# Loads of v in 20 and 10 columns, stores in pairs of pieces, and a new order for both

## The chip, the cores and the metric

The kernel runs on one core of a Trainium2 chip. The metric is the device time of one execution in microseconds; the median of several runs is given, and one further execution was profiled. TensorE is called PE here, VectorE DVE, ScalarE ACT, GpSimd POOL and SyncE SP.

## The reference

Four batches of channel attention (the attention matrix is 256 x 256, over channels), followed by a mixture of eight low-rank adapters of which each token uses two. The tokens are N = 6,400 per batch, C = 256 channels, r = 16.

```python
qn = q / (norm(q, axis=1) + 1e-06)            # q, k, v: (4, 6400, 256) f32, norms over tokens
kn = k / (norm(k, axis=1) + 1e-06)
s  = kn.transpose(0, 2, 1) @ qn / tau         # (4, 256, 256)
a  = softmax(s, axis=-1)
x  = (v @ a).reshape(25600, 256)
logits = x @ w_gate                           # (25600, 8); the two largest per token
w = softmax(of the two)
out = x + sum over the two of w * ((x @ A[e]) @ B[e])
```

The output is 25,600 x 256 in f32.

## The kernel before

**Tiling.** The tokens of a batch are laid out as 128 partitions x 50 columns; a column is 128 tokens x 256 channels. q and k of a batch come in three loads each, of 17, 17 and 16 columns (`QK`); some are cut finer (`PARTS`). v of a batch is worked on in five pieces of ten columns (`PC`, `NP`), each with its own load. All these loads turn f32 into bf16 on the way and are issued by POOL (`do_load`, L627). The first four columns of q and k of batch 0 come as f32 from SP and ACT.

**Stages.** For each batch, PE accumulates over the 50 columns the Gram matrix of k and q and, beside it, the squares that the norms need (`G`, L642, L646, L651). Groups of columns named in `OFF` have their squares made on ACT and added on DVE instead (`sq`, `add`, `red`, L664 to L679). Then come the norms, the softmax and the product of its matrix with gate and adapter weights (`rsqrt` to `a`). Only then can a piece of v be finished: PE transposes it (`T`, L828), makes the gate logits (`log`, L866) and, behind the gate chain on DVE, the adapter product (`Z`, L919), or both at once where the piece is in `MERGED` (`ZL`, L852). The gated product is transposed (`gzT`, L942), and the output `Y` is made two columns at a time (L955, L960), copied to SBUF by ACT or DVE (`Ye`) and stored by SP (`do_store`, L971).

**Buffers.** `STORE` lists them: six buffers for q and k loads, three pieces of v side by side in one tile `VS`, four transposed pieces (`vT`), seven pieces of output in one tile `Y`, six PSUM banks for the stages, three sets of gate tiles. A load waits until every user of its buffer has finished, and the loads on POOL go out in the order written in `WORDS` (a word is q and k, or v, then the batch, then the part). A store may also be made to wait until a certain load has landed: `HOLD` names, for a piece, that load (batch, part; for v the piece). SP's queue is in order.

**Order.** The order on each engine is made when the kernel is built: `make_plan` writes down all steps with their dependences, their costs and a rank (the place of their load in `WORDS`; `AHEAD` and `SQ` shift ranks), and `Plan.run` plays them through with those costs and takes on each engine the best-ranked step that is ready. `Clock` is its notion of PE's clock; where PE would be idle, it puts `warm` matmuls (L818). The result is a fixed sequence for each engine. `V`, `PAIRS` and `SPLIT` are already in the code, but neutral: `V` has five loads of one piece for each batch, and the two others are empty.

Of the kernel before, what the change touches and what calls it, by code (L numbers as in the profile page):

```python
# [10 lines left out]
FP32 = mybir.dt.float32  # L11
I32 = mybir.dt.int32
BF16 = mybir.dt.bfloat16
# [19 lines left out]
class Clock:  # L33


    WINDOW, FIRST, LOW, HIGH = 3.413, 0.31, 0.55, 0.8

    def __init__(self):
        self.busy, self.cold = [0.0], [True]
# [23 lines left out]
        w = self.at(t)  # L63
        return t - self.FIRST - (w - 1) * self.WINDOW - self.busy[w] > self.SPARE

    SPARE = 0.8


class Plan:
# [171 lines left out]
PC = 10  # L241
NP = 5
UNITS = ((0, 4), (4, 4), (8, 2))
QK = ((0, 17), (17, 17), (34, 16))
V = (((0, 1), (1, 1), (2, 1), (3, 1), (4, 1)),) * 4
PAIRS = set()

GROUPS = ((0, 6), (6, 6), (12, 5), (17, 6), (23, 6), (29, 5), (34, 6), (40, 5), (45, 5))
ZUNITS = ((0, 3), (3, 3), (6, 2), (8, 2))
STORE = {"zl": 1, "bank": 6, "qk": 6, "v": 3, "vT": 4, "y": 7, "gate": 3, "gz": 4, "gzT": 4, "sq": 1, "ssq": 2, "port": 1}  # L250


def group_of(c):
# [187 lines left out]
def make_order(words):  # L441

    order = [("qk", 0, i) for i in range(len(QK))]
    for w in words.split():
# [1 line left out]
    return order  # L446


WORDS = ('q10 v00 v01 v02 q11 q12 v03 v04 v10 q20 v11 v12 q21 v13 q22 v14 q30 q31 v20 v21 v22 q32 v23 v24 v30 '
         'v31 v32 v33 v34')  # L450
HEAD = 5.05
COL = 1.024 * 1.17647 / 32
WARM = 150
AHEAD = 2.8

HOLD = {(0, 0): ('k', 2, 0), (0, 1): ('v', 3, 4), (0, 3): ('v', 2, 3), (1, 0): ('v', 3, 1), (1, 1): ('v', 3,
        1), (1, 3): ('v', 2, 3), (1, 4): ('v', 3, 0), (2, 2): ('v', 3, 2), (2, 3): ('v', 0, 4), (3, 0):
        ('k', 3, 2), (3, 1): ('k', 1, 1), (3, 2): ('v', 0, 1), (3, 4): ('k', 2, 1)}

PARTS = {(0, 0): ((0, 4), (4, 13)), (0, 2): ((34, 8), (42, 8)), (3, 2): ((34, 8), (42, 8))}  # L460
FINE = 2
SPLIT, SHARES = set(), ()
OFF = {(0, 0, 'k'), (0, 1, 'q'), (0, 2, 'q'), (0, 3, 'q'), (0, 5, 'q'), (0, 6, 'k'), (0, 8, 'k'), (1, 0,
        'k'), (1, 1, 'k'), (1, 2, 'k'), (1, 2, 'q'), (1, 3, 'q'), (1, 4, 'k'), (1, 5, 'q'), (1, 6, 'k'), (1,
        6, 'q'), (2, 0, 'k'), (2, 0, 'q'), (2, 3, 'q'), (2, 5, 'k'), (2, 5, 'q'), (2, 6, 'k'), (2, 7, 'q'),
        (2, 8, 'q'), (3, 0, 'k'), (3, 0, 'q'), (3, 1, 'q'), (3, 2, 'k'), (3, 2, 'q'), (3, 4, 'q'), (3, 5,
        'k'), (3, 6, 'k'), (3, 6, 'q'), (3, 7, 'k'), (3, 8, 'k')}
SQ = 0
SAFE = 0
MERGED = {(0, 1), (0, 4), (1, 0), (2, 1), (2, 2), (3, 0), (3, 2), (3, 3)}  # L470


def first_ahead(nc, names):
# [31 lines left out]
def kernel(  # L505
# [58 lines left out]
    def make_consts():  # L564
        ident = const.tile([P, P], BF16, name="ident")
        make_identity(nc, ident)
        W["ident"] = ident
        W["ident32"] = const.tile([P, P], FP32, name="ident32")
        nc.vector.tensor_copy(W["ident32"], ident)
        ones = const.tile([P, P], FP32, name="ones")  # L570
        nc.vector.memset(ones, 1.0)
        W["ones"] = ones
        neg = const.tile([P, 1], FP32, name="neg_inv_tau")
        nc.vector.memset(neg, -inv_tau)
        W["neg"] = neg
        W["zeros"] = const.tile([P, 256], BF16, name="zeros")
        nc.vector.memset(W["zeros"], 0.0)
        nc.scalar.activation(scrap[:, 0:1], neg[0:1, :], ACT.Exp)

    scrap = const.tile([1, 16], BF16, name="scrap")  # L580
# [128 lines left out]
    def do_rsqrt(s, b):  # L709
        n2 = st[b]["n2"]  # L710
        for x, w in enumerate("kq"):
            part = held.get(("bank", ("n2p", w, b)))
            if part is None:
                continue
            if all((b, g, w) in OFF for g in range(len(GROUPS))):
                nc.vector.tensor_copy(n2[:, x, :], part)
            else:
                nc.vector.tensor_tensor(out=n2[:, x, :], in0=part, in1=n2[:, x, :], op=OP.add)

        r = bat.tile([P, 2, CC], FP32, name="r0")  # L720
        nc.vector.tensor_scalar(out=r.bitcast(I32), in0=n2.bitcast(I32), scalar1=-0.5,
                                scalar2=float(0x5F1FFFF9), op0=OP.mult, op1=OP.add)
        for it, (c1, c0) in enumerate(((-0.703952253, 1.681914351), (-0.5, 1.5))):
            sq = bat.tile([P, 2, CC], FP32, name=f"sq{it}")
            nc.vector.tensor_tensor(out=sq, in0=r, in1=r, op=OP.mult)
            nc.vector.scalar_tensor_tensor(out=sq, in0=sq, scalar=c1, in1=n2,
                                           op0=OP.mult, op1=OP.mult)
            nxt = bat.tile([P, 2, CC], FP32, name=f"r{it + 1}")
            nc.vector.scalar_tensor_tensor(out=nxt, in0=sq, scalar=c0, in1=r,
                                           op0=OP.add, op1=OP.mult)  # L730
            r = nxt
        rqI = one.tile([P, CC, P], FP32, name="rqI")
        for ic in range(CC):
            nc.vector.tensor_scalar(out=rqI[:, ic, :], in0=W["ident"],
                                    scalar1=r[:, 1, ic:ic + 1], scalar2=None, op0=OP.mult)
        if inv_tau != 1.0:
            rt = bat.tile([P, CC], FP32, name="rt")
            nc.vector.tensor_scalar(out=rt, in0=r[:, 0, :], scalar1=inv_tau, scalar2=None, op0=OP.mult)
            st[b]["rk"] = rt
        else:  # L740
            st[b]["rk"] = r[:, 0, :]
        st[b]["rqI"] = rqI
# [72 lines left out]
        nc.scalar.copy(held["qk", (what, 0, 0), ""][:, 0:PARTS[0, 0][0][1], :], W[what])  # L815

    def do_warm(s, n):
        nc.tensor.matmul(bank(s, ("warm", n), [P, 512], FP32), W["ident"], W["zeros"][:, None, :].to_broadcast([P, 2, 256]),  # L818
                         start=True, stop=True)


# [16 lines left out]


    def gate_tiles(s, b, i):  # L840
        for part in ("log", "eq1", "lm", "t", "th", "mask", "g2"):
            sb(s, "gate", (b, i), [P, PC, E], FP32, part)
        for part in ("m1", "m2", "msum"):
            sb(s, "gate", (b, i), [P, PC], FP32, part)
# [30 lines left out]
    def gate_step(name):  # L875
        def f(s, b, i):
            if (b, i) in MERGED and name == "m1":
                gate_tiles(s, b, i)
            g = {part: held["gate", (b, i), part]
                 for part in ("log", "m1", "eq1", "lm", "m2", "msum", "t", "th", "mask", "g2")}  # L880
            if (b, i) in MERGED:
                g["log"] = held["zl", (b, i), ""][:, :, 0:E]
            wide = [P, PC, E]
            if name == "m1":
                nc.vector.tensor_reduce(out=g["m1"], in_=g["log"], axis=AX.X, op=OP.max)
            elif name == "eq1":
                nc.vector.tensor_tensor(out=g["eq1"], in0=g["log"], in1=g["m1"].to_broadcast(wide),
                                        op=OP.is_equal)
            elif name == "lm":
                nc.vector.scalar_tensor_tensor(out=g["lm"], in0=g["eq1"], scalar=-1e30, in1=g["log"],  # L890
                                               op0=OP.mult, op1=OP.add)
            elif name == "m2":
                nc.vector.tensor_reduce(out=g["m2"], in_=g["lm"], axis=AX.X, op=OP.max)
            elif name == "mask":
                nc.vector.tensor_tensor(out=g["mask"], in0=g["log"], in1=g["m2"].to_broadcast(wide),
                                        op=OP.is_ge)
            elif name == "msum":
                nc.vector.tensor_tensor(out=g["msum"], in0=g["m1"], in1=g["m2"], op=OP.add)
            elif name == "t":

                nc.vector.scalar_tensor_tensor(out=g["t"], in0=g["log"], scalar=2.0,
                                               in1=g["msum"].to_broadcast(wide),
                                               op0=OP.mult, op1=OP.subtract)
            elif name == "th":
                nc.scalar.activation(g["th"], g["t"], ACT.Tanh, scale=0.5)
            else:

                nc.vector.scalar_tensor_tensor(out=g["g2"], in0=g["th"], scalar=1.0, in1=g["mask"],
                                               op0=OP.add, op1=OP.mult)
        return f  # L910
# [13 lines left out]
    def do_Ze(s, b, i, u):  # L924
        c, n = UNITS[u]
        gz = sb(s, "gz", (b, i, u), [P, n, ER], BF16)
        z = held["zl", (b, i), ""][:, c:c + n, E:] if (b, i) in MERGED else held["bank", ("Z", b, i, u)]
        pairs = gz.rearrange("p c d -> p (c d)").rearrange("p (h x two) -> p h two x", two=2, x=ER)
        for h in range(n // 2):
            nc.vector.tensor_tensor(  # L930
                out=pairs[:, h].rearrange("p c (e r) -> p c e r", e=E),
                in0=z[:, 2 * h:2 * h + 2, :].rearrange("p c (e r) -> p c e r", e=E),
                in1=held["gate", (b, i), "g2"][:, c + 2 * h:c + 2 * h + 2, :].to_broadcast([P, 2, E, R]), op=OP.mult)

    def do_gzT(s, b, i, u):
        c, n = UNITS[u]
# [98 lines left out]
```

## Time and profile before

| | |
|---|---|
| median of 4 runs | 254.55 us (254.31 to 254.83) |
| profiled execution | 254.28 us, its span 252.5 us |
| granted PE clock, mean | 0.966 |
| PE busy | 221.2 us (88%) |
| DVE busy | 170.8 us (68%) |
| ACT busy | 158.4 us (63%) |
| loads by POOL (q0) | 38.80 MB written, 74.6% of 16 engines |
| stores by SP (q1) | 26.87 MB with the first pieces, 26.0% |
| HBM | 78.91 MB read, 26.21 MB written |

The time of an execution is a little more than its span, which runs from the first to the last instruction. A DMA share is the busy time of the 16 DMA engines; a load counts the bytes that it writes (bf16), so loads alone show about 215 GB/s and stores alone about 425.

### The profile page before, as it was taken

Reading aid. Unit: us, or ns where it says so; the run is one execution under the profiler, and the core shown is the slowest. Engines: PE = TensorE matmul, PEld = TensorE weight load, DVE = VectorE, ACT = ScalarE, POOL = GpSimd, SP = SyncE. Lnnn points to the kernel's source line nnn. Section 1 sums busy time; section 2 is a strip of 40 time slices with the busy share of each in tenths; the row PEclk is TensorE's granted clock in tenths of the full one; section 3 lists DMA queues with packets and bytes.
Section 4 is the critical chain, followed back from the end, with each engine's and each line's share of the span. In section 5 each row is a group of like instructions: output and inputs, shape, how many; then the busy total and the mean of one; then the engine's idle time right before and its main releaser. Section 6 shows DMA issues by size and latency. Waiting matters only on the chain.

```text
span 252.5 us, 6005 instructions
## 1 busy us (share of the span) xinstructions
PE 221.2 (88%) x2467; PEld 196.9 (78%) x2467; DVE 170.8 (68%) x485; ACT 158.4 (63%) x294; POOL 26.7 (11%) x54
## 2 busy tenths in 40 slices
PE   0775995899999899999998998899998889999970
PEld 0463883699899898889997997699978879999960
DVE  0024386169996988786749679879996797598430
ACT  5324123366877758767774778756953958877760
POOL 7003011011000201000101203010000110000000
PEclk9978899599999999999999999999999999999997
DMA  8999999999999999999999999999999999999995
GB/s 251 214 216 212 212 222 210 215 219 216 215 211 219 306 222 210 316 292 243 220 212 301 234 219 216 207 213 215 214 302 405 423 244 303 346 378 425 426 413 235
DMA packets 11147, 66.71 MB, mean 264 GB/s; under 512 B 1264, under 2 KB 1648, under 8 KB 6512
## 3 DMA queue, kind: packets, MB, share of 16 engines
q0 software_dynamic: 6912, 38.80, 74.6%
q1 hardware_dynamic: 3872, 26.87, 26.0%
q10 hardware_dynamic: 336, 0.66, 0.8%
q8 instruction: 19, 0.31, 0.4%
q14 instruction: 8, 0.07, 0.1%
HBM read 78.91 MB, written 26.21 MB: 416 GB/s over the span
## 4 chain that ended last, share of the span: by engine, by line
PE 56%; DMA 26%; DVE 9%; ACT 4%; issue 1%; POOL 0%; POOLq 0%; DVEq 0%
DMA qk<-in_k_dram 14%; PE Y_ps L955 14%; PE acc L642 8%; PE Y_ps L960 7%; DMA v<-in_v_dram 7%; PE T_ps L828 6%; DMA out_dram<-y 5%; PE gzT_ps L942 4%; PE Z_ps L919 4%; DVE ssq L670 4%; PE ZL_ps L852 3%; PE acc L646 2%; ACT sq L664 2%; PE acc L651 2%; PE log_ps L866 2%
## 5 line engine op out<-in xcount | busy, mean ns | idle before, releaser
L642 PE MATMUL acc<-qk 128*128 128x256 bf16 x400 | 74.8, 285 | 15.7 <-DMA qk<-in_k_dram 9.5
L955 PE MATMUL Y_ps<-a_bf,vT 128*128 128x256 bf16 x400 | 60.0, 272 | 0.9 <-ACT y L810 0.9
L670 DVE TENSOR_TENSOR ssq<-ssq,sq 128x1280 f32<-128x1280 f32 (+1 forms) x27 | 43.3, 1604 | 25.4 <-ACT sq L664 25.1
L810 ACT COPY y<-Y_ps 128x512 f32<-128x512 f32 x83 | 48.0, 588 | 18.8 <-PE Y_ps L960 12.0
L664 ACT ACTIVATE sq<-qk 128x1280 f32<-128x1280 bf16 (+1 forms) x27 | 36.9, 1368 | 28.1 <-DVE ssq L670 9.9
L642 PEld LDWEIGHTS <-qk 128*128 128x128 bf16 x400 | 35.8, 103 | 20.3 <-DMA qk<-in_k_dram 11.0
L955 PEld LDWEIGHTS <-vT 128*128 128x128 bf16 x400 | 38.7, 99 | 5.3 <-issue 1.0
L960 PE MATMUL Y_ps<-ball,gzT 128*128 128x256 bf16 x200 | 38.2, 273 | 0.0
L646 PE MATMUL acc<-qk 128*128 128x128 bf16 x210 | 30.0, 225 | 0.0
L651 PE MATMUL acc<-qk 128*128 128x128 bf16 x200 | 29.0, 229 | 0.0
L828 PE MATMUL T_ps<-ident,v 128*128 128x128 f32 x200 | 28.4, 277 | 0.0
L930 DVE TENSOR_TENSOR gz<-Z_ps,gateg 128x256 bf16<-128x256 f32 x60 | 22.4, 440 | 4.3 <-PE Z_ps L919 4.1
L810 ACT COPY vT<-T_ps 128x512 f32<-128x512 f32 (+1 forms) x43 | 21.7, 540 | 5.2 <-PE T_ps L828 4.9
L646 PEld LDWEIGHTS <-qk 128*128 128x128 bf16 x210 | 21.2, 101 | 3.0
L828 PEld LDWEIGHTS T_ps<-ident,v 128*128 128x128 f32 x200 | 22.5, 143 | 0.4 <-issue 0.2
L810 ACT COPY gzT<-gzT_ps 128x256 f32<-128x256 f32 (+1 forms) x45 | 14.7, 347 | 11.7 <-PE gzT_ps L942 11.6
L627 POOL DMA_DIRECT2D v<-in_v_dram x20 | 11.1, 553 | 102.4 <-PE T_ps L828 88.5
L960 PEld LDWEIGHTS <-gzT 128*128 128x128 bf16 x200 | 19.5, 98 | 2.5 <-DVE gzT L812 0.3
L942 PE MATMUL gzT_ps<-ident,gz 128*128 128x128 f32 x100 | 19.7, 281 | 1.4 <-DVE gz L930 1.0
L651 PEld LDWEIGHTS <-qk 128*128 128x128 bf16 x200 | 18.9, 103 | 2.4
L919 PE MATMUL Z_ps<-waA_sb,vT 128*128 128x128 bf16 x240 | 17.7, 219 | 0.0
L664 ACT ACTIVATE ssq<-qk 128x1536 f32<-128x1536 bf16 x8 | 11.9, 1486 | 8.4 <-DMA qk<-in_k_dram 4.3
(80 smaller groups left out, 274.0 us busy)
## 6 DMA issues: line engine op xcount, KB each, us to landing
out_dram<-y SPq DMA_DIRECT2D x18, 1280.0 KB, 12.6
v<-in_v_dram POOLq DMA_DIRECT2D x20, 640.0 KB, 25.1
qk<-in_q_dram POOLq DMA_DIRECT2D x7, 1088.0 KB, 22.2
qk<-in_k_dram POOLq DMA_DIRECT2D x7, 1088.0 KB, 26.8
qk<-in_q_dram POOLq DMA_DIRECT2D x4, 512.0 KB, 23.0
qk<-in_k_dram POOLq DMA_DIRECT2D x4, 512.0 KB, 24.7
qk<-in_q_dram POOLq DMA_DIRECT2D x2, 1024.0 KB, 30.9
qk<-in_k_dram POOLq DMA_DIRECT2D x2, 1024.0 KB, 35.2
```

What stands on the lines that cost most here:

```text
L642: nc.tensor.matmul(acc[ic][:, 0:256], kt[:, j, ic::CC], qt[:, j, :], start=c == 0, stop=False, skip_group_check=True)
L646: nc.tensor.matmul(acc[ic][:, 256:384], kt[:, j, ic::CC], kt[:, j, ic::CC], start=False, stop=False, skip_group_check=True)
L651: nc.tensor.matmul(acc[ic][:, 384:512], qt[:, j, ic * P:(ic + 1) * P], qt[:, j, ic * P:(ic + 1) * P], start=False, stop=c == NC - 1, skip_ ...
L664: nc.scalar.activation(out[:, 0:n, :], t[:, j:j + n, :], ACT.Square)
L670: nc.vector.tensor_tensor(out=t, in0=t, in1=held["sq", (w, b, g), ""][:, 0:n, :], op=OP.add)
L810: nc.scalar.copy(out, in_)
L828: nc.tensor.matmul(ps[:, j, :], vt[:, c + j, :].bitcast(FP32), W["ident32"], is_transpose=True, start=(j == 0), stop=(j == n - 1))
L919: nc.tensor.matmul(ps[:, j, :], vT_of(b, i, c + j)[:, :, ic], st[b]["aA"][:, ic, :], start=(j == 0 and ic == 0), stop=(j == n - 1 and ic = ...
L930: nc.vector.tensor_tensor(out=pairs[:, h].rearrange("p c (e r) -> p c e r", e=E), in0=z[:, 2 * h:2 * h + 2, :].rearrange("p c (e r) -> p c ...
L942: nc.tensor.matmul(ps[:, j, :], pairs[:, j * P:(j + 1) * P], W["ident32"], is_transpose=True, start=(j == 0), stop=(j == n // 2 - 1))
L955: nc.tensor.matmul(ps[:, j, :], vT_of(b, i, c + j)[:, :, ic], st[b]["a"][:, ic, :], start=(j == 0 and ic == 0), stop=False, skip_group_che ...
L960: nc.tensor.matmul(ps[:, j, :], pair[:, :, j], W["B"], start=False, stop=(j == 1), skip_group_check=True)
```

## The change

v is loaded in 15 transfers instead of 20: five of them bring two pieces (20 columns) into two adjacent buffers of `VS`, which now has four. Ten pieces are stored in five transfers of two pieces. Pieces named in `SPLIT` are stored in four shares of 112, 6, 6 and 4 partitions. The order of loads (`WORDS`), the loads that stores wait for (`HOLD`), the split of the squares between PE and ACT (`OFF`: 189 columns instead of 195), the merged pieces (`MERGED`: 14 instead of 8) and the parameters of the planner (`LOW`, `SPARE`, `AHEAD`, `SQ`, `SAFE`) have new values, so that every engine's sequence is new. The room for the fourth v buffer comes from gate tiles that now share two buffers (`GATE`), from the tile `zeros` (the warm matmuls read `ident` instead) and from `rqI`, which takes the place of `ssqk`.

The transfers in their order, as both kernels issue them (q means the pair q and k; v12+13 is one transfer of two pieces):

```
loads before  q00 q01 q02 q10 v00 v01 v02 q11 q12 v03 v04 v10 q20 v11 v12 q21 v13 q22 v14
              q30 q31 v20 v21 v22 q32 v23 v24 v30 v31 v32 v33 v34
loads after   q00 q01 q02 q10 v00 v01+02 q11 q12 v03+04 q20 q21 v10 q22 v11 v12+13 v14
              q30 q31 v20 v21 v22 q32 v23 v24 v30+31 v32+33 v34
stores before 02 00 04 12 20 03 13 14 21 10 11 22 23 24 30 01 31 32 33 (3 parts) 34 (3 parts)
stores after  00+01 04 (4 shares) 14 02+03 20 10+11 12+13 21+22 23 24 30 31 (4 shares) 32
              33 and 34 (3 parts each, interleaved)
```

The instruction counts that follow: PE 29 warm matmuls before, 21 after; `log` and `Z` for 12 pieces before, 6 after.

The diff, with the two lists of `OFF` cut:

```diff
@@ -33,7 +33,7 @@
 class Clock:
 
 
-    WINDOW, FIRST, LOW, HIGH = 3.413, 0.31, 0.55, 0.8
+    WINDOW, FIRST, LOW, HIGH = 3.413, 0.31, 0.45, 0.8
 
     def __init__(self):
         self.busy, self.cold = [0.0], [True]
@@ -63,7 +63,7 @@
         w = self.at(t)
         return t - self.FIRST - (w - 1) * self.WINDOW - self.busy[w] > self.SPARE
 
-    SPARE = 0.8
+    SPARE = 1.0
 
 
 class Plan:
@@ -241,13 +241,15 @@
 PC = 10
 NP = 5
 UNITS = ((0, 4), (4, 4), (8, 2))
+GATE = {"eq1": "ga", "t": "ga", "th": "ga", "g2": "ga", "lm": "gb", "mask": "gb"}
 QK = ((0, 17), (17, 17), (34, 16))
-V = (((0, 1), (1, 1), (2, 1), (3, 1), (4, 1)),) * 4
-PAIRS = set()
+V = (((0, 1), (1, 2), (3, 2)), ((0, 1), (1, 1), (2, 2), (4, 1)), ((0, 1), (1, 1), (2, 1), (3, 1), (4, 1)),
+        ((0, 2), (2, 2), (4, 1)))
+PAIRS = {(0, 0), (0, 2), (1, 0), (1, 2), (2, 1)}
 
 GROUPS = ((0, 6), (6, 6), (12, 5), (17, 6), (23, 6), (29, 5), (34, 6), (40, 5), (45, 5))
 ZUNITS = ((0, 3), (3, 3), (6, 2), (8, 2))
-STORE = {"zl": 1, "bank": 6, "qk": 6, "v": 3, "vT": 4, "y": 7, "gate": 3, "gz": 4, "gzT": 4, "sq": 1, "ssq": 2, "port": 1}
+STORE = {"zl": 1, "bank": 6, "qk": 6, "v": 4, "vT": 4, "y": 7, "gate": 3, "gz": 4, "gzT": 4, "sq": 1, "ssq": 2, "port": 1}
 
 
 def group_of(c):
@@ -446,28 +448,29 @@
     return order
 
 
-WORDS = ('q10 v00 v01 v02 q11 q12 v03 v04 v10 q20 v11 v12 q21 v13 q22 v14 q30 q31 v20 v21 v22 q32 v23 v24 v30 '
-         'v31 v32 v33 v34')
+WORDS = ('q10 v00 v01 q11 q12 v02 q20 q21 v10 q22 v11 v12 v13 q30 q31 v20 v21 v22 q32 v23 v24 v30 v31 v32')
 HEAD = 5.05
 COL = 1.024 * 1.17647 / 32
 WARM = 150
-AHEAD = 2.8
-
-HOLD = {(0, 0): ('k', 2, 0), (0, 1): ('v', 3, 4), (0, 3): ('v', 2, 3), (1, 0): ('v', 3, 1), (1, 1): ('v', 3,
-        1), (1, 3): ('v', 2, 3), (1, 4): ('v', 3, 0), (2, 2): ('v', 3, 2), (2, 3): ('v', 0, 4), (3, 0):
-        ('k', 3, 2), (3, 1): ('k', 1, 1), (3, 2): ('v', 0, 1), (3, 4): ('k', 2, 1)}
+AHEAD = 4.3
+
+HOLD = {(0, 1): ('k', 1, 2), (0, 2): ('v', 2, 4), (0, 3): ('v', 3, 2), (0, 4): ('v', 2, 1), (1, 0): ('v', 3,
+        0), (1, 1): ('k', 3, 0), (1, 2): ('v', 3, 1), (2, 0): ('v', 0, 0), (2, 2): ('k', 3, 0), (2, 3):
+        ('k', 2, 1), (3, 0): ('v', 1, 0), (3, 1): ('v', 2, 1), (3, 2): ('v', 3, 3), (3, 3): ('k', 2, 2), (3,
+        4): ('v', 1, 4)}
 
 PARTS = {(0, 0): ((0, 4), (4, 13)), (0, 2): ((34, 8), (42, 8)), (3, 2): ((34, 8), (42, 8))}
 FINE = 2
-SPLIT, SHARES = set(), ()
-OFF = {(0, 0, 'k'), (0, 1, 'q'),
...
-SQ = 0
-SAFE = 0
-MERGED = {(0, 1), (0, 4), (1, 0), (2, 1), (2, 2), (3, 0), (3, 2), (3, 3)}
+SPLIT, SHARES = {(0, 4), (2, 2), (3, 1)}, (112, 6, 6, 4)
+OFF = {(0, 0, 'k'), (0, 1, 'k'),
...
+SQ = 2.5
+SAFE = 0.2
+MERGED = {(0, 0), (0, 3), (0, 4), (1, 0), (1, 1), (1, 2), (1, 3), (1, 4), (2, 2), (2, 3), (3, 0), (3, 1),
+        (3, 2), (3, 4)}
 
 
 def first_ahead(nc, names):
@@ -573,8 +576,6 @@
         neg = const.tile([P, 1], FP32, name="neg_inv_tau")
         nc.vector.memset(neg, -inv_tau)
         W["neg"] = neg
-        W["zeros"] = const.tile([P, 256], BF16, name="zeros")
-        nc.vector.memset(W["zeros"], 0.0)
         nc.scalar.activation(scrap[:, 0:1], neg[0:1, :], ACT.Exp)
 
     scrap = const.tile([1, 16], BF16, name="scrap")
@@ -729,7 +730,7 @@
             nc.vector.scalar_tensor_tensor(out=nxt, in0=sq, scalar=c0, in1=r,
                                            op0=OP.add, op1=OP.mult)
             r = nxt
-        rqI = one.tile([P, CC, P], FP32, name="rqI")
+        rqI = one.tile([P, CC, P], FP32, tag="ssqk", name="rqI")
         for ic in range(CC):
             nc.vector.tensor_scalar(out=rqI[:, ic, :], in0=W["ident"],
                                     scalar1=r[:, 1, ic:ic + 1], scalar2=None, op0=OP.mult)
@@ -815,7 +816,7 @@
         nc.scalar.copy(held["qk", (what, 0, 0), ""][:, 0:PARTS[0, 0][0][1], :], W[what])
 
     def do_warm(s, n):
-        nc.tensor.matmul(bank(s, ("warm", n), [P, 512], FP32), W["ident"], W["zeros"][:, None, :].to_broadcast([P, 2, 256]),
+        nc.tensor.matmul(bank(s, ("warm", n), [P, 512], FP32), W["ident"], W["ident"][:, None, :].to_broadcast([P, 4, P]),
                          start=True, stop=True)
 
 
@@ -838,7 +839,7 @@
 
 
     def gate_tiles(s, b, i):
-        for part in ("log", "eq1", "lm", "t", "th", "mask", "g2"):
+        for part in ("log", "ga", "gb"):
             sb(s, "gate", (b, i), [P, PC, E], FP32, part)
         for part in ("m1", "m2", "msum"):
             sb(s, "gate", (b, i), [P, PC], FP32, part)
@@ -876,7 +877,7 @@
         def f(s, b, i):
             if (b, i) in MERGED and name == "m1":
                 gate_tiles(s, b, i)
-            g = {part: held["gate", (b, i), part]
+            g = {part: held["gate", (b, i), GATE.get(part, part)]
                  for part in ("log", "m1", "eq1", "lm", "m2", "msum", "t", "th", "mask", "g2")}
             if (b, i) in MERGED:
                 g["log"] = held["zl", (b, i), ""][:, :, 0:E]
@@ -930,7 +931,7 @@
             nc.vector.tensor_tensor(
                 out=pairs[:, h].rearrange("p c (e r) -> p c e r", e=E),
                 in0=z[:, 2 * h:2 * h + 2, :].rearrange("p c (e r) -> p c e r", e=E),
-                in1=held["gate", (b, i), "g2"][:, c + 2 * h:c + 2 * h + 2, :].to_broadcast([P, 2, E, R]), op=OP.mult)
+                in1=held["gate", (b, i), "ga"][:, c + 2 * h:c + 2 * h + 2, :].to_broadcast([P, 2, E, R]), op=OP.mult)
 
     def do_gzT(s, b, i, u):
         c, n = UNITS[u]
```

## The prediction

> **What bounds the kernel now.** I read the page's slices first, then the windows of the middle, the tail and the stage around the last softmax, then the chain and the POOL queue's waits.
>
> ```profile
> span 252.5 us, 6005 instructions
> PE 221.2 (88%) x2467; PEld 196.9 (78%) x2467; DVE 170.8 (68%) x485; ACT 158.4 (63%) x294; POOL 26.7 (11%) x54
> DMA  8999999999999999999999999999999999999995
> ...
> q0 software_dynamic: 6912, 38.80, 74.6%
> q1 hardware_dynamic: 3872, 26.87, 26.0%
> ...
> 45.00:245.00 200.00, 192.45 (x2215) 174.62 (x2215) 153.79 (x442) 142.84 (x280) 16.86 (x31) 0.98 1.03 274
> ...
> 240.00:244.00 4.00, 4.00 (x43) 3.48 (x42) 1.96 (x5) 2.53 (x6) 0.00 (x0) 1.00 1.00 418
> 244.00:248.00 4.00, 0.71 (x7) 0.39 (x4) 0.00 (x0) 1.20 (x3) 0.00 (x0) 1.00 1.01 411
> 248.00:252.00 4.00, 0.00 (x0) 0.00 (x0) 0.00 (x0) 0.00 (x0) 0.00 (x0) 0.63 0.46 182
> ...
> POOL v L627 <- PE T_ps L828: 88.5, 14, 26.0
> ...
> 165.52 17.61 DMA v<-in_v_dram
> 183.15 12.92 DMA out_dram<-y
> 196.08 0.59 ACT y L810
> ```
>
> The DMA row is full from the first slice to the last but one; loads (q0) and stores (q1) together fill 16 engines for the span. PE is busy 192.45 of 200 us between 45 and 245, but its last matmul ends at 244.8 while the stores run at 411 GB/s until 248: the end is transfers, PE close behind. The last wait row says that v's transfers wait for PE to empty a buffer: harmless while others are queued. The chain's three lines show PE, at the third softmax's end, waiting for v and then for a place in y.
>
> What a transfer costs is read from the trace's packet records, as the time between the completion marks of consecutive transfers: a load with 8,704 B rows 5.17 us, 5,120 B (ten columns of v) 3.06, 4,096 B 2.46, a ten-column store 3.05. The three loads lie on 0.05 us + 0.588 us per 1,000 B of row. Sum: loads 14 x 5.17 + 4 x 4.87 + 8 x 2.46 + 2 x 3.97 + 20 x 3.06 = 180.7; stores 20 x 3.05 = 61.0; first pieces and weights about 3.1; 19 instruction fetches of 16 KB, 0.93 each on one engine, and smaller ones 1.4 over 16. That is 246.2 us. The first packet moves at 1.0 and the engines finish between 249.8 and 251.2 (marks of the last store, mean 250.4): 249.4 us for 246.2 of work. So no schedule can gain much; each us without a queued transfer costs one.
>
> **The change part by part.**
>
> *Fewer, larger transfers.* v goes from 20 loads to 15 (five pairs), stores from 20 pieces to 15 (five pairs). Bytes are the same. By the fit a pair saves one fixed 0.05 us: 5 x 0.05 = 0.25 us on every engine. For stores 4,096 B rows (about 1.2 us) against 10,240 B (3.05) leave next to nothing: 0. No 20-column transfer is in the trace; were its rows cut in two, it would cost what two do. Row against rule: the Trainium skill (DMA: Bandwidth & Descriptors, "Anatomy of one DMA") gives a transfer about 2 us fixed plus its bytes. Ten fewer would give 20 us. But the marks 3.06 us apart contain no 2 us: here that cost is latency behind a queue (loads land 25.1 us after issue in the median). I take 0.25.
>
> *Split stores.* Pieces (0,4) and (3,1) go out in rows 112, 6, 6, 4; (2,2) is named too, but as a pair's second half is stored with (2,1), unsplit. Here a rule speaks against the change: the same page ("Why a DMA increments its semaphore by 16") says that a transfer from this queue runs on the largest number of engines up to 16 that divides its outer size, the lowest-numbered. 112 rows give 7 to each engine, 6 rows one to each of engines 0-5, 4 rows one to 0-3. A row is 3.05 / 8 = 0.38 us. Over two stores engines 0-3 get four rows more (+1.52), 4 and 5 two more (+0.76), the other ten two fewer (-0.76). By an even spread the sum would be 0; by the rule the slow engines decide. No 6-row transfer is in the trace. What it shows is the marks of the last full store but one: six engines finish at 238.84 to 239.79, ten at 240.5 to 241.81. Six lead by 2.0 to 3.0 us, since the fetches fall on the others. If those six are 0-5, which the trace cannot say, the end moves by -0.76; if not, by +1.52. Their lead at the last mark has shrunk to 0.8-1.5 (some idled waiting for the last stores), so I count -0.6.
>
> *PE.* MERGED grows from 8 to 14 pieces: each swaps 20 log and 20 Z matmuls (0.48 + 1.12) for 20 ZL (1.18 to 1.34): -0.26 to -0.42, six times -1.6 to -2.5. OFF falls from 195 to 189 columns: 6 x 2 x 0.055 = +0.7. Warm matmuls fall from 29 to 21, at 0.22 to 0.43 each; they fill idle time, and count 0, but with them gone PE's clock could be halved in a gap (0.50 in 45-50 already); before the first softmax the new order has five in a row. PE needs 1 to 2 us less; hidden under the DMA.
>
> *ACT and DVE.* Six more ZL evictions per piece set: ACT zl copies 505 and 407 ns, about 1.8 us a piece against 0.22 for log: +9.5 us over two engines that have 82 and 94 us free; one norm step less (-1.3 and -1.5). Hidden under PE. The shared gate buffers ga and gb follow a chain that is serial already; rqI in ssqk's place is written after PE has read ssqk. 0. The dropped 128x256 memset: 0, in the head.
>
> *Order and waits.* In the old order four stores leave by 142 us; in the new one a single pair does before v(2,1) has landed, so loads run ahead by 12.2 - 6.1 = 6.1 us from there. Is POOL allowed to issue them in time? New start of movement = 5.6 (start and first pieces) + loads ahead + 6.1 (pair) + 1 (fetches); beside it, the time at which the old trace already had the buffers free (its issue):
>
> - q of (3,0): 132.3; issued 123.0
> - q of (3,1): 142.6; 137.6
> - v(2,0), v(2,1): 153; 138.9
> - q of (3,2): 162; 152.9
> - v(2,3), v(2,4): 172 and 175; 165.5 and 168.5
>
> The tightest has 5.0 us, 3 after the latency of issue. The new PE order puts the releasing steps earlier (batch 2's 34th column before Y of piece (1,1), not behind that of (1,2)), and a fourth v buffer loosens T's grip, the 88.5 us above. So the DMA stays fed: 0. A pair lands whole: v(0,1) is usable 3.06 us later; PE then has q(1,0)'s 17 columns and piece (0,0). The pairs' stores wait for a second piece and keep two of seven places in y longer.
>
> *SP's queue* is in order: behind the store of (0,4), which waits for v(2,1), stand all others; y holds nine pieces until it lands (seven, and the first pair's two places again), so piece (1,4) waits for it.
>
> Sum: 252.5 - 0.25 - 0.6 = 251.65; the execution took 254.28 for its 252.5, so 253.4; the median of the runs is 0.27 above it: **253.7 us**.
>
> **The rivals.**
>
> *A, no change:* the split helps nothing or costs as much as the larger transfers save: 254.55 - 0.25 to + 0.3, 254.3 to 254.9. For: the last mark's small spread. Against: the spread 10 us earlier.
>
> *B, slower, PE starves for y:* the new order stores less early, and PE must finish by about 247.5 (last matmul 244.8, last store issued at 246.1, and landed 5.1 us later where an unqueued one would need about 2.3, so 2.8 us of slack), to which PE's saving adds 1.5. The place: piece (1,4), for which (0,4) must be stored, and later the pair (2,1)-(2,2), for which the pair (0,2)-(0,3) must. If each store takes the median 12.6 us to land instead of the 5.5 that I allow, PE loses 7 us twice, of which it can make up half with T and ZL of other pieces: 7 - 4.3 = +2.7, 257. It decides from 4.3 us of lost PE time on. For: the 12.92 us line of the chain is just this wait. Against: PE still ended before the stores.
>
> *C, slower, the six leaders are other engines:* 254.55 + 1.52 - 0.25 = 255.8. For: nothing in the trace numbers the engines. Against: the shares add rows to exactly six engines, and exactly six lead.
>
> *D, the fixed cost is real:* ten fewer transfers at up to 2 us, 245 or less: excluded by 246.2 us of packet work.
>
> **How the numbers follow.** Forecast (251 to 254.0) 0.45; A 0.20, of which some falls just under the bound; B 0.22; C 0.12; D 0.01. What a measurement can tell from no change is about 0.2%, 0.5 us: faster is under 254.04, slower over 255.06. Faster 0.46, same 0.19, slower 0.35. The range goes from 252.8 (the full 0.76 and 1 us of less idle DMA) to 256.6, most of the way to B; the likeliest case alone has 252.9 to 254.0.
>
> **What would show it.** Right: the DMA row is full as before; completion marks of a 20-column load 6.07 us apart and of a store 6.1; the ten late engines' marks at the last store come about 1 us earlier; PE's last matmul before 246; the last load of batch 3's q and k lands some 6 us earlier than 179. Wrong: a slice of DMA below 9 between 100 and 180 (a load issued late); PE's last matmul after 247.5 with "ACT y <- DMA out_dram<-y" grown from 4.5 us (B); the last store's marks spread by more than 2 us with full slices (C).

## The result: slower by a third of a per cent

The changed kernel takes 255.19 us in the median of 35 runs (254.18 to 257.96), the kernel before 254.54 (254.18 to 255.20, 54 runs): ratio 1.0034, 95% interval 1.0022 to 1.0046 (the ratio follows the means; of the medians it is 1.0026). Forecast was 253.7 and a gain. The range held the time, the sign was wrong. Two things stand out before any experiment: the fastest execution is no faster than before, and single executions are nearly 3 us slower than the median, which the kernel before never shows. The ratios leave out two executions far slower than the others of their kernel, one of 586 us and one of 264.55, which the medians below include.

The page of the changed kernel, its first lines and the two large queues (packets, MB, share of 16 engines):

```profile
span 252.6 us, 5793 instructions
...
PE 220.7 (87%) x2351; PEld 194.2 (77%) x2351; DVE 174.8 (69%) x498; ACT 157.6 (62%) x296; POOL 23.6 (9%) x49
...
DMA  8999999999999999999999999999999999999995
...
q0 software_dynamic: 6192, 38.80, 74.1%
q1 hardware_dynamic: 3184, 26.87, 25.9%
```

The DMA row is as full as before, PE and the stores are as busy, and the packets are fewer because rows of 20 columns are single packets. The profiled execution took 254.37 us, less than the median, so the loss is small in it. The windows from 45 on (busy us of PE, PEld, DVE, ACT, POOL; granted PE clock, DMA share, GB/s):

```profile
45.00:245.00 200.00, 192.41 (x2128) 173.59 (x2128) 157.89 (x470) 139.50 (x280) 14.31 (x27) 0.99 1.03 275
...
234.00:240.00 6.00, 6.00 (x64) 5.53 (x62) 4.23 (x15) 5.06 (x12) 0.00 (x0) 1.00 0.99 400
240.00:244.00 4.00, 4.00 (x39) 3.60 (x37) 0.68 (x2) 3.27 (x6) 0.00 (x0) 1.00 0.99 402
244.00:248.00 4.00, 0.62 (x6) 0.31 (x4) 0.00 (x0) 1.17 (x2) 0.00 (x0) 0.92 1.02 410
248.00:252.00 4.00, 0.00 (x0) 0.00 (x0) 0.00 (x0) 0.00 (x0) 0.00 (x0) 0.50 0.38 150
```

From 240 to 244 us the stores move at 402 GB/s, where the kernel before had 418. The engines are reported busy (0.99), so it is not that work is missing: packets take longer. In the packet records, 25 store packets of 10,240 B after 225 us take over 430 ns (8 before), where the ordinary one takes 385; together they are 5.4 us too long (1.2 before), and single ones take 900. That is little over 16 engines, but an execution ends with its last engine: by the completion counter of the last store, which counts a mark from each engine, its sixteen marks have a mean of 249.89 us, earlier than before (250.16), while the last of them is at 251.72 (251.57 before).

### The profile page after: what moved, and what is told of

Its sections match the earlier page's. It is cut to its first block, busy times and chain, and to the rows that moved or that the text cites. A ratio compares the mean times of both kernels' runs of the same rounds, so it can differ in the third digit from the quotient of the medians.

```text
span 252.6 us, 5793 instructions
## 1 busy us (share of the span) xinstructions
PE 220.7 (87%) x2351; PEld 194.2 (77%) x2351; DVE 174.8 (69%) x498; ACT 157.6 (62%) x296; POOL 23.6 (9%) x49
## 4 chain that ended last, share of the span: by engine, by line
DMA 47%; PE 31%; DVE 10%; ACT 5%; issue 2%; POOL 2%; SPq 0%; POOLq 0%; ACTq 0%; DVEq 0%
DMA qk<-in_k_dram 22%; DMA v<-in_v_dram 21%; PE Y_ps L956 9%; PE Y_ps L961 5%; DMA out_dram<-y 4%; PE acc L643 3%; PE T_ps L829 3%; PE ZL_ps L853 3%; DVE ssq L671 3%; ACT sq L665 2%; PE gzT_ps L943 2%; PE Z_ps L920 2%; ACT a_exp L757 1%; PE acc L652 1%; POOL qk L628 1%
## 5 line engine op out<-in xcount | busy, mean ns | idle before, releaser
L671 DVE TENSOR_TENSOR ssq<-ssq,sq 128x1280 f32<-128x1280 f32 (+1 forms) x26 | 41.6, 1600 | 27.4 <-ACT sq L665 27.4
L811 ACT COPY y<-Y_ps 128x512 f32<-128x512 f32 x80 | 45.4, 590 | 12.8 <-PE Y_ps L961 7.5
L665 ACT ACTIVATE sq<-qk 128x1280 f32<-128x1280 bf16 (+1 forms) x26 | 35.5, 1365 | 19.0 <-DVE ssq L671 10.4
L956 PEld LDWEIGHTS <-vT 128*128 128x128 bf16 x400 | 38.7, 98 | 4.4 <-issue 0.2
L811 ACT COPY vT<-T_ps 128x512 f32<-128x512 f32 (+1 forms) x45 | 22.9, 548 | 18.4 <-PE T_ps L829 18.2
L652 PE MATMUL acc<-qk 128*128 128x128 bf16 x224 | 33.2, 233 | 0.0
L829 PE MATMUL T_ps<-ident,v 128*128 128x128 f32 x200 | 26.2, 274 | 3.0 <-DMA v<-in_v_dram 2.1
L647 PE MATMUL acc<-qk 128*128 128x128 bf16 x198 | 27.5, 219 | 0.0
L931 DVE TENSOR_TENSOR gz<-zl,gatega 128x256 bf16<-128x256 f32 x70 | 26.0, 447 | 0.4
L853 PE MATMUL ZL_ps<-waA_sb,vT 128*128 128x136 bf16 x280 | 20.6, 222 | 0.4
L853 PEld LDWEIGHTS <-vT 128*128 128x128 bf16 x280 | 18.0, 98 | 1.9 <-issue 0.9
L813 DVE COPY zl<-ZL_ps 128x272 f32<-128x272 f32 (+1 forms) x20 | 9.7, 496 | 11.2 <-PE ZL_ps L853 11.2
```

Of the source, the lines that this page charges most:

```text
L647: nc.tensor.matmul(acc[ic][:, 256:384], kt[:, j, ic::CC], kt[:, j, ic::CC], start=False, stop=False, skip_group_check=True)
L652: nc.tensor.matmul(acc[ic][:, 384:512], qt[:, j, ic * P:(ic + 1) * P], qt[:, j, ic * P:(ic + 1) * P], start=False, stop=c == NC - 1, skip_ ...
L665: nc.scalar.activation(out[:, 0:n, :], t[:, j:j + n, :], ACT.Square)
L671: nc.vector.tensor_tensor(out=t, in0=t, in1=held["sq", (w, b, g), ""][:, 0:n, :], op=OP.add)
L811: nc.scalar.copy(out, in_)
L829: nc.tensor.matmul(ps[:, j, :], vt[:, c + j, :].bitcast(FP32), W["ident32"], is_transpose=True, start=(j == 0), stop=(j == n - 1))
```

## The experiments

Each kernel ran with the kernel before on the same chip; the ratios are to that. Where the packet records are counted, "long packets" are store packets of 10,240 B that start after 225 us and take over 430 ns, and their excess is the sum of what they take beyond 385 ns.

### Is it the shares, and where

First the changed kernel again, beside the same without the shares, the kernel before with them, and the changed kernel without the hold that stood for rival B.

**The changed kernel again** (no edit).

> The changed kernel itself, timed beside the other three on one chip, for their comparison and for a second profile. If its time depends on chance within the run (the 35 executions so far lie between 254.18 and 257.96, those of the kernel before between 254.18 and 255.20), the median comes out at 255.2 again, give or take 0.3, with single executions above 256. A second profile in which PE's last matmul ends after 245.5 and the store of piece (0,4) lands later than 172.4 would speak for rival B (PE starved for places in y).

Measured 254.98 us (254.39 to 258.20), ratio 1.0020 (1.0005 to 1.0034). The spread is there again. The second profile has PE's end where the first has it, and 28 long packets with an excess of 7.9 us.

**The changed kernel without shares.**

```diff
-SPLIT, SHARES = {(0, 4), (2, 2), (3, 1)}, (112, 6, 6, 4)
+SPLIT, SHARES = set(), ()
```

> The changed kernel with SPLIT empty: pieces (0,4) and (3,1) leave in one transfer each; PE's sequence is untouched. Forecast of the recorded prediction (the ten slow engines profit from the shares): 0.6 slower than the changed kernel, 255.8. Rival C (the shares burden the wrong engines): 1 to 1.5 faster, 254.0. Rival B: the four shares lie on the chain at 160.9 to 162.0 (SP issues three more transfers before (0,4) has wholly left); without them the store lands up to 1 us earlier and PE gets on earlier, 254.7, and the spread of the executions shrinks a little.

Measured 253.62 us (253.59 to 253.89), ratio 0.9964 (0.9950 to 0.9977): 1.4 us faster than the changed kernel beside it, and faster than the kernel before. The rest of the change does what was forecast for the whole; the shares turn it round. Repeated later:

> The changed kernel without shares again, for a narrower interval (five executions so far) and beside the early share on one chip: 253.6, ratio 0.9965, executions within 253.4 to 254.2.

Measured 253.72 (253.43 to 255.12), ratio 0.9965 (0.9947 to 0.9983). This version beats both kernels. The tail of the first of these two runs:

```profile
234.00:240.00 6.00, 6.00 (x63) 5.51 (x62) 4.23 (x15) 5.05 (x12) 0.00 (x0) 1.00 1.02 428
240.00:244.00 4.00, 4.00 (x39) 3.59 (x38) 0.49 (x2) 3.26 (x7) 0.00 (x0) 1.00 0.98 410
244.00:248.00 4.00, 0.43 (x4) 0.14 (x2) 0.00 (x0) 0.99 (x2) 0.00 (x0) 1.00 0.99 397
248.00:252.00 4.00, 0.00 (x0) 0.00 (x0) 0.00 (x0) 0.00 (x0) 0.00 (x0) 0.68 0.30 120
```

Against the lines of the changed kernel above, the six microseconds from 234 on, while piece (3,1) is leaving, have 428 GB/s instead of 400, with PE's column unchanged; afterwards less is left to move (120 against 150 GB/s in the last stretch). 7 long packets, excess 0.7.

**The kernel before with shares.**

```diff
-SPLIT, SHARES = set(), ()
+SPLIT, SHARES = {(0, 4), (3, 1)}, (112, 6, 6, 4)
```

> The kernel before with the four shares for pieces (0,4) and (3,1), nothing else changed. This measures the shares alone, in a kernel whose time hardly varies. Recorded forecast: the ten slow engines carry two rows of 0.38 us less, 254.54 - 0.6 = 253.9; in the profile the last marks of the stores lie closer together. Rival C: the leaders are not engines 0 to 5, 254.54 + 1.5 = 256.0, last marks spread over more than 2 us. Rival A: 254.5, within 0.3.

Measured 257.84 us (255.44 to 259.25), ratio 1.0119 (1.0079 to 1.0158): 3.3 us slower, more than twice what rival C said. The number of completion marks on the store queue grows from 416 to 448, by 16 for each piece: 6 + 6 + 4, as the rule of the Trainium skill has it (DMA: Bandwidth & Descriptors, "Why a DMA increments its semaphore by 16"). By the counter of the last store, twelve marks come from 250.01 to 251.28 and four from 252.67 to 255.83. 52 long packets, excess 16.4.

**The changed kernel, store of (0,4) not held.**

```diff
-            if (b, i) in HOLD and not p:
+            if (b, i) in HOLD and (b, i) != (0, 4) and not p:
```

> The changed kernel, but the store of piece (0,4) no longer waits for v(2,1) to land: it leaves as soon as its columns are copied, in the same place of SP's order; all else is the same. Rival B (PE waits for a place in y behind this store, chain at 162.0 to 172.5): the place comes free tens of us earlier, the wait of 10.4 us leaves the chain, the high executions go, 254.3. If PE's feed by loads is what varies instead, moving 3 us of store ahead of loads makes it worse: 256.5. If neither: unchanged, 255.2.

Measured 254.91 us (254.32 to 255.73), ratio 1.0016 (1.0004 to 1.0027): the same as the changed kernel beside it. The wait is real. In the chain of the changed kernel SP's three share issues and the landing stand ahead of a copy into y:

```profile
160.88 0.34 SPq L972
161.22 0.05 issue
161.27 0.37 SPq L972
161.64 0.05 issue
161.69 0.27 SPq L972
161.96 0.04 issue
162.00 10.40 DMA out_dram<-y
172.40 0.03 DVEq L813
172.44 0.04 issue
172.48 0.70 DVE y L813
```

With the hold gone, no DMA stands in the chain between 150 and 184 us and PE is busy 19.99 of the 20 us from 155 to 175 (19.10 with it); yet PE's last matmul then ends later (after 246.0 instead of 244.6) and the time is what it was. Rival B's place was right, its price was not: it is hidden. The highest of these 14 executions is 255.73, where three of 22 of the changed kernel beside it lie at 256.0 or above; so few do not tell whether the hold adds to the spread.

### Row counts, the cut by rows, or the number of transfers

Three theories were left for the shares: the uneven counts (I), the cut by rows itself (M), and the number of transfers (Q). All these kernels are the kernel before with one edit.

**Even counts: shares of 112 and 16** (`SPLIT, SHARES = {(0, 4), (3, 1)}, (112, 16)`).

> The kernel before with pieces (0,4) and (3,1) stored in shares of 112 and 16 rows. By the rule for the engine count both shares run on all 16 engines, 7 rows and 1 row each: the row counts stay even[...]. Theory I (uneven row counts are what costs): 254.6, as before. Theory M (the seven-row mapping makes engines meet at the same partitions; in the profile of the kernel before with four shares store packets of 10,240 B take 700 to 1,500 ns around 236 to 245 instead of 385): most of the 3.3 us stays, 257. Theory Q (each further transfer costs SP's queue and a completion): one extra transfer for a piece instead of three, 255.6.

Measured 255.32 us, ratio 1.0034 (1.0023 to 1.0046). The counts are even, and it still costs. 36 long packets, excess 14.6. Theory I alone is out. The kernel before from 234 to 240 (its next line stands in the prediction), then this one:

```profile
234.00:240.00 6.00, 6.00 (x61) 5.50 (x59) 2.59 (x10) 4.91 (x10) 0.00 (x0) 1.00 1.01 423
```

```profile
234.00:240.00 6.00, 6.00 (x66) 5.54 (x64) 2.34 (x9) 4.91 (x10) 0.00 (x0) 1.00 1.01 383
240.00:244.00 4.00, 4.00 (x40) 3.28 (x37) 1.69 (x5) 2.53 (x6) 0.00 (x0) 1.00 0.99 386
```

**Only the early piece** (`SPLIT = {(0, 4)}`, four shares).

> The kernel before with shares 112, 6, 6, 4 for piece (0,4) alone, which is stored at about 110 to 120 us. Theory I: half of the imbalance, engines 0-3 carry two rows more (+0.76), kept to the end since the DMA is never idle: 255.3. Theory M: no effect, since loads run beside that store and its packets were not slow: 254.6. Theory Q: no effect, 254.6.

Measured 254.43 us, ratio 0.9990 (0.9982 to 0.9998): a small gain, where the recorded working would give 0.38 us for one piece, if the six engines lead. 9 long packets, excess 1.2: as in the kernel before. The packets of the cut store itself, at 111 to 123 us beside loads, take 398 ns in the median as without the cut, one of them over 430.

**Only the late piece** (`SPLIT = {(3, 1)}`, four shares).

> The kernel before with shares 112, 6, 6, 4 for piece (3,1) alone, stored at about 236 us when only stores move. Theory I: as for the early one, 255.3; the two add up to the 3.3 us only if the tail amplifies. Theory M: nearly all of the 3.3 us, 257.5, with the slow packets at 236 to 245 as before. Theory Q: three transfers more in the tail, where eight stores in flight are the limit of SP's completion counters: 256.

Measured 255.37 us (254.60 to 257.84), ratio 1.0032 (1.0015 to 1.0050). 32 long packets, excess 10.7. The windows of the two, first the early piece, then the late one:

```profile
234.00:240.00 6.00, 6.00 (x64) 5.52 (x62) 2.31 (x10) 4.84 (x11) 0.00 (x0) 1.00 1.00 419
240.00:244.00 4.00, 4.00 (x43) 3.45 (x41) 1.92 (x5) 2.53 (x6) 0.00 (x0) 1.00 1.00 419
```

```profile
234.00:240.00 6.00, 6.00 (x65) 5.53 (x64) 2.32 (x9) 4.90 (x10) 0.00 (x0) 1.00 1.00 388
240.00:244.00 4.00, 4.00 (x41) 3.35 (x38) 1.76 (x5) 2.53 (x6) 0.00 (x0) 1.00 0.99 396
```

The same shares cost nothing while loads run beside the store, and 5 to 7% of the rate where only stores move, with the DMA share unchanged.

**Two transfers, cut by columns.** The same two pieces leave in two transfers of five columns, 128 rows each:

```diff
-        for rows in SHARES if (b, i) in SPLIT else (P,):
-            r = nc.sync.dma_start(out_v[b, p:p + rows, lo:lo + n, :], Y[p:p + rows, at_y:at_y + n, :])
+        parts = ((0, n // 2), (n // 2, n - n // 2)) if (b, i) in SPLIT else ((0, n),)
+        for o, m in parts:
+            r = nc.sync.dma_start(out_v[b, :, lo + o:lo + o + m, :], Y[:, at_y + o:at_y + o + m, :])
```

> The kernel before with pieces (0,4) and (3,1) stored in two transfers of five columns each, all 128 rows in both: one extra transfer for a piece as with the shares of 112 and 16 rows, but the ordinary eight rows for each engine. Theory Q (extra transfers cost): 255.3, as the shares of 112 and 16 did (ratio 1.0034). Theory M (it is the cut by rows): 254.6, ratio 1.000, and no slow store packets at 236 to 245.

Measured 254.58 us, ratio 0.9992 (0.9980 to 1.0005), 7 long packets with an excess of 1.2. Its 5,120 B packets take at most 256 ns after 225 us, 196 in the median. One extra transfer costs nothing: theory Q is out for it.

```profile
234.00:240.00 6.00, 6.00 (x64) 5.52 (x62) 2.31 (x10) 4.84 (x11) 0.00 (x0) 1.00 1.01 421
240.00:244.00 4.00, 4.00 (x42) 3.45 (x40) 1.85 (x5) 2.53 (x6) 0.00 (x0) 1.00 1.01 423
```

**Three late pieces in 112 and 16** (`SPLIT, SHARES = {(3, 0), (3, 1), (3, 2)}, (112, 16)`).

> The kernel before with pieces (3,0), (3,1) and (3,2) stored in shares of 112 and 16 rows, all three in the last 25 us. Row counts stay even. Theory M: three times the late cost that one of them has (0.6 to 0.8 us): 256.6 to 257, and the transfer rate between 228 and 244 falls to about 385 GB/s all along instead of 420. Theory I: 254.6.

Measured 260.83 us, ratio 1.0213 (1.0165 to 1.0261): 5.4 us by the ratio, and still with equal counts. It grows faster than the number of pieces. The rates are read from the next two kernels, which cut the same three pieces.

**Which share: 64 and 64, and 112 alone** (the same three pieces, `SHARES = (64, 64)` and `SHARES = (112,)`).

> The kernel before with pieces (3,0), (3,1) and (3,2) stored in two shares of 64 rows each: four rows for each engine in both, so counts are even, there is no share of 16 neighbouring rows and no seven-row step. Theory M1 (only the seven-row step, or only the narrow 16-row share, is slow): 254.6, no slow packets. Theory M2 (any share that is not the whole 128 rows makes engines read partitions that are others' in the ordinary spread): as with 112 and 16, 258 or more, slow packets all through 228 to 250.

Measured 259.55 us, ratio 1.0181 (1.0138 to 1.0224), 83 long packets with an excess of 25.8.

> The kernel before with only 112 of the 128 rows of pieces (3,0), (3,1) and (3,2) stored; the last 16 partitions of these three pieces are left out of the output, so 3 x 0.38 us of store are missing on every engine: about 253.5 where nothing else changes. Theory M1a (the narrow 16-row share is the slow one): 253.5, few packets above 430 ns after 225. Theory M1b or M2 (the seven-row step is the slow one): 258 or more, with slow packets as in the kernel with both shares (126 of them after 225 us).

Measured 257.02 us, ratio 1.0093 (1.0069 to 1.0116), though an eighth of three stores is left out; 104 long packets, excess 32.2. First 64 and 64, then 112 alone:

```profile
240.00:244.00 4.00, 3.98 (x38) 3.15 (x34) 1.55 (x5) 2.51 (x5) 0.00 (x0) 1.00 0.96 364
244.00:248.00 4.00, 0.00 (x0) 0.00 (x0) 0.00 (x0) 0.58 (x1) 0.00 (x0) 1.00 0.91 322
```

```profile
240.00:244.00 4.00, 4.00 (x44) 3.48 (x42) 1.96 (x5) 2.53 (x6) 0.00 (x0) 1.00 1.00 336
244.00:248.00 4.00, 0.57 (x6) 0.26 (x3) 0.00 (x0) 1.12 (x2) 0.00 (x0) 1.00 0.99 380
```

So it is neither the narrow share nor the seven-row step alone: each of the cuts of the 128 rows that was tried, 112 + 16, 64 + 64 and 112 alone, is slow. With 112 alone there is not even an extra transfer. PE's column is what it is in the kernel before (4.00 us from 240 to 244), and the rate falls from 418 to 336 GB/s with 112 alone.

**What SP shows.** The instruction on SP that issues a store also takes longer behind such a cut. Its count, its shortest, median and longest duration in ns, and its first and last start, for the kernel before, two transfers cut by columns, 112 alone, and 64 and 64:

```profile
L971 SPq DMA_DIRECT2D out_dram<-y x24: 332/332/1037, 78.1 to 245.4; - x24
L971 SPq DMA_DIRECT2D out_dram<-y x26: 332/332/854, 77.7 to 244.9; - x26
L971 SPq DMA_DIRECT2D out_dram<-y x24: 327/343/2453, 78.0 to 247.1; - x24
L971 SPq DMA_DIRECT2D out_dram<-y x27: 332/490/2363, 77.8 to 248.3; - x27
```

The last copy into y ends at 245.3, 244.9, 245.2 and 244.6 us. In the first two kernels the last store is issued at once; behind the cuts by rows it waits 1.9 and 3.7 us more, while the four issues just ahead of it take 1.1 to 2.5 us each. The changed kernel has the same trait in small: its last three issues take 0.92, 0.85 and 1.16 us, without shares 0.33 to 0.49. What holds up an issue is not on record. With 64 and 64 the DMA share falls to 0.91, so engines do run short of work there; with 112 alone it stays at 0.99 or more, so there the late issue is more likely an effect of the slow packets than the cause of the loss.

### What carries the gain of the rest

**Paired loads as two transfers**, in the changed kernel without shares:

```diff
-        loaded[s.key] = nc.gpsimd.dma_start(t[:, 0:n, :], src[b, :, c:c + n, :]).ins.name
+        step = PC if what == "v" else n
+        for o in range(0, n, step):
+            loaded[s.key] = nc.gpsimd.dma_start(t[:, o:o + step, :], src[b, :, c + o:c + o + step, :]).ins.name
```

> The changed kernel without shares (253.62), but each of the five 20-column loads of v is issued as two of ten columns, one behind the other; all sequences of PE, ACT, DVE and SP stay. Recorded prediction: 5 x 0.05 us more on every engine, 253.9. If larger transfers carry more of the gain of 0.96 (fewer fixed costs than the packets show): 254.3 or more. If they carry none: 253.6.

Measured 254.10 us, ratio 0.9979 (0.9971 to 0.9987), against 0.9964 for the pairs, on another chip: 0.15% or 0.4 us, with intervals that overlap. The forecast term was 0.25.

**Paired stores as two transfers**, in the same kernel: `do_store` issues 20 columns as twice ten, the hold on the first.

> The changed kernel without shares, but each of the five 20-column stores is issued as two of ten columns, one behind the other, held by the same load; all else stays. Recorded prediction: stores of pairs save next to nothing, so 253.7, ratio 0.9965. If a good part of the 1.0 us that the kernel without shares gains comes from them (fewer completions, or two pieces' places in y freed otherwise): 254.0 or more.

Measured 254.16 us, ratio 0.9984 (0.9976 to 0.9993) against 0.9964 and 0.9965: about 0.5 us, where the forecast had 0; the interval touches those of the paired kernel, which ran on other chips. The packet records point the same way: the store queue's packets take 64.92 us for each of 16 engines in the kernel without shares and 65.52 with these stores cut in two, the load queue's 187.27 and, with the loads cut in two, 188.13 (packets overlap, so this is more than the time that it costs). If the two terms add up, they make most of the 0.9 us by which the kernel without shares beats the kernel before; they were not taken out together.

**The early share in the changed kernel** (`SPLIT = {(0, 4)}`).

> The changed kernel with the four shares for piece (0,4) alone, the one stored while loads still run; (3,1) leaves whole. If the recorded forecast's step on the leading engines is right where loads run beside the store (in the kernel before this share alone gave a ratio of 0.999): 253.3, a little below the 253.6 of no shares, the lowest of all. If any shares cost in this kernel, whose next step waits for this very store: 254.3.

Measured 253.99 us, ratio 0.9969 (0.9958 to 0.9980), no different from no shares at all (0.9965 on the same chip). 5 long packets, excess 0.7. It is no gain here and no loss; as (2,2) is not cut, the loss of the changed kernel is that of the late piece, (3,1).

## Why the prediction was wrong

**The step that failed is "Split stores", counted as -0.6 us.** It weighed rows per engine at a fixed 0.38 us a row. With even counts, where that working gives 0, the shares of 112 and 16 cost as much (ratio 1.0034) as the late four shares alone (1.0032); the price of a row is what changed. In the tail, where only stores move, a cut by rows makes some store packets two to four times as long. In the changed kernel the shares cost 1.4 us (1.0020 against 0.9964 on one chip) instead of gaining 0.6: that is the sign of the whole result.

**A reading behind that step was wrong too.** The prediction took the last sixteen marks of the store queue for those of the last store and found the lead of six engines shrunk to 0.8 to 1.5 us. Those sixteen belong to more than one store. By the counter of the last store alone, six marks of the kernel before come from 248.43 to 249.49 and ten from 250.16 to 251.57: the lead on the last mark is 2.1 to 3.1 us, as at (3,1). So the sign that was set for rival C, marks spread by more than 2 us, tells nothing: they spread by 3.1 us before, 3.3 after, and 3.3 without shares.

**Why a cut by rows is slow** was not settled. The Trainium skill (DMA: Bandwidth & Descriptors, "The descriptor swizzle") says of a transfer of all 128 partitions into SBUF that each engine writes partitions behind one port; a store reads them. If shares spread their rows otherwise, engines would meet at a port; that fits all these runs, and that it shows only at the full store rate. But no record tells ports, or SBUF from HBM, so it is an argument and not shown. Open too is why both pieces in the kernel before cost 1.19% and the two alone -0.10% and 0.32%.

**Rival A** came closest in number (254.9 at most, 0.3 us off) and in form: it had the split cost as much as the larger transfers save. The split cost 1.4 us, and the rest saved 0.9.

**Rival C** (255.8) was wrong in its cause: equal counts cost as well. Its reason, that the six engines with extra rows do not lead, has something for it. The marks of a six-row share are those of its six engines, and with the late piece alone cut they come at 239.2, 240.0, 240.2, 241.1, 241.6 and 243.9 us, where those of the 112 rows go from 238.8 to 243.2: one of the six seems to be the last of all. With both pieces cut, the marks of the four-row share come at 240.5, 241.3, 241.4 and 245.4, so that of the four engines with the most extra rows three are not late. The early share gave 0.3 us in the kernel before, near the 0.38 that leaders would give, and none in the changed kernel.

**Rival B** named a wait that the chain then showed, 10.40 us at piece (1,4); taking its hold away moved the time by 0.07 us of 255. PE ended at 244.6, within the slack that the prediction had given (about 247.5).

**Larger transfers, -0.25.** Right in sign and near in the packets: without shares, a 20-column load completes 6.07 to 6.14 us behind the one ahead of it, two of ten take 6.12 to 6.19; taking the pairs of loads apart cost about 0.4. The whole, without shares, gains 0.9, of which stores seem to carry more than the 0 that was put down: that term measured about 0.5, with a wide interval.

**Order, 0.** Right: no slice of the DMA row falls, and every load was issued before the load ahead of it had landed. Not right in size: batch 3's last q and k landed 3 us earlier than before, not 6, because the store of (0,4) is freed by v(2,1), which lands ahead of them, and so moves beside them. PE, ACT and DVE at 0: their busy times moved by under 5 us, and in the changed kernel PE's last matmul ends 7 us before the last mark.

**Rival D** (2 us for each transfer) is out, as the prediction had it: the changed kernel without shares has ten transfers fewer and gains 0.9 us, not 20. The section that the prediction cites for the 2 us is on transfers that GpSimd issues, and five of the ten are SP's.

## What to carry to other kernels

Keep a store over all 128 partitions, and divide it by columns where it has to be divided: cutting the same two pieces by columns was free, by rows it cost 0.3% to 1.2%, and nothing for the piece that left while loads ran beside it. Before a plan moves rows between DMA engines, measure one such transfer in the stretch where it will run: here the price of a row in a whole transfer did not hold for a share. Read the marks of a transfer by its own completion counter, since the order of time mixes those of neighbours. When a change bundles a schedule, larger transfers and a trim of the tail, take the trim out first: here that alone turned a loss of 0.20% into a gain of 0.36%, on one chip.

## What the runs showed of the hardware

Where only stores move, the 10,240 B packets of stores of all 128 rows take 385 ns (398 beside loads). In the tail of kernels with a late piece cut by rows, most packets kept that time, but 20 to 104 took over 430 ns (8 before), the longest 0.96 to 1.9 us, and the rate between 234 and 248 us, 411 to 423 GB/s in the kernel before, fell to as low as 322 with 64 and 64 and 336 with 112 alone. The DMA share was 0.91 to 1.04 meanwhile: the share of busy time does not tell good packets from long ones. The same shares with loads beside them left the packets alone. Issuing a store took SP 0.33 us in the median, and up to 2.5 us behind such a cut. With the shares the executions of one kernel also spread further: 254.2 to 258.2 us for the changed kernel (57 executions), 253.4 to 255.1 without shares (15).
